# One table for the whole kernel: global queries in batches of four pairs, routed values in pairs of query blocks, gate weights split on the chip

## The chip, the cores and the metric

The kernel runs on one core of one Trainium2 chip. The metric is the time of one execution in device microseconds (us); lower is better. A core has a matrix engine (PE, with PEld for its weight loads), a vector engine (DVE), a scalar engine (ACT), GpSimd (POOL), and DMA queues, of which nearly all are issued from SyncE (SP). Each engine runs its own instructions in the order in which the program lists them, and waits where an input or a buffer is not ready.

## The reference, cut to what matters

Three layers follow each other. First an attention with 512 local and 32 global positions (4 batches, 8 heads of 64): local queries see a band of 32 positions to each side and all global keys, global queries see everything.

```
s_g = scale * np.matmul(q_g, k_all.transpose(0, 1, 3, 2))
out_g = np.matmul(sm(s_g), v_all)
...
a_l = sm(concatenate([s_lg, where(mask, s_ll, -1e9)]))
out_l = np.matmul(a_l, np.concatenate([v_g, v_l], axis=2))
```

Then a routed layer of four causal attention experts (two per token, weighted by a softmax of gate logits), and last a channel mix with a sigmoid gate:

```
scores = where(causal, -1e9, scale * (q @ k.T)); a = softmax(scores)
ye = a @ v @ wo[e]
...
k = np.maximum(xk @ w_k, 0.0)
v = k * k @ w_v
r = 1.0 / (1.0 + np.exp(-(xr @ w_r)))
return (r * v).astype(np.float32)
```

The inputs of `w_k`, `w_v` and `w_r` come as 64-bit floats, and the kernel makes 32-bit ones of them itself.

## The kernel before, in words

Large matrix products are made of three passes in a fast float format (fp32r): each operand is kept as a high part H and a rest L. Small products (scores and values of the attention, values of the experts, transposes) are plain fp32, and each such matmul stands as two records in the trace.

**Attention (tiles S, pn, pT, x).** Sixteen pairs of heads are loaded as `kq` (queries and keys, 688 KB, four buffers) and `vw` (values). `a_qk` makes scores `S` of a half pair in four 64x64 parts of the array, DVE and ACT make the softmax `sm`, POOL scales it to `pn`, PE transposes it (`pT`), and `a_pv` multiplies by the values into `x`. Two pairs make a unit u, two units a batch b. `g_qk(u)` makes the scores `Sga` and `Sgb` of the global queries, four heads side by side in four strips of 32 output partitions; `g_norm` and `g_tp` scale and transpose them into `plg` or `ptlg`. Their product with the values (`xg`) stands inside `a_pv`: every value block that is loaded as weights for `x` serves a 32-column matmul for `xg` too.

**Routed layer (tiles x, pb, pv, C, csm, cT, y, po).** `b_*` project, `c_qk` and `c_norm` make the scaled scores `csm` of one expert pair ep and one block i of 128 queries, `c_tp` transposes them (`cT`) into a buffer `cpt` (two of them), `c_pv` multiplies by the values into `y`, and `e_wo` projects back (`po`). `l_*` do the same for the last 32 positions of all batches.

**Channel mix (tiles m0, m1, k, kk, v, r, rt).** Five tiles of tokens (four of 512, one of 128); per tile 96 matmuls of 512 columns for k, 96 for v and 48 for r. `split_wd` narrows a 64-bit weight chunk with two ACT, one POOL and three DVE instructions, then splits it into H (ACT) and L (POOL). For `w_v` and `w_r` the parts are written to DRAM during the routed layer (`dv..`, `dr..`) and fetched again when their place in SBUF is free (`fetch_wd`).

All calls are first logged; `emit` then issues them by a table of numbers (`ORDER`), and a second table (`SLOTS`) says which buffer each tile takes. So the order on every engine, SP's queue among them, is written out by hand in these tables. The profile has nearly all instructions at the one line of `emit` (L104), so that they are told apart by the names of tiles.

Of the kernel before, what the change touches and what calls it, by code (L numbers as in the profile page):

```python
# [116 lines left out]
def chain_kernel(ctx: ExitStack, tc: tile.TileContext, kq, vw, vgd, wqkv, pack, wo, w_k, w_v, w_r, c_causal, out):  # L117
# [10 lines left out]
    BUFS = {"W0": 1, "W1": 1, "W2": 1, "x": 1, "qk": 3, "kp": 4, "raw": 2, "wy": 2, "wg": 2, "csm0": 4, "csm1": 2,  # L128
            "cpt": 2, "vC": 2, "y": 2, "wo": 2, "pl": 1, "ptl": 1, "rep": 2, "ql": 1}
# [52 lines left out]
    def mm3_rows(ops):  # L182

        for n, (a, x) in enumerate(((1, 3), (1, 4), (2, 3))):
# [8 lines left out]
           for name, k in (("v", 0), ("v", 1), ("r", 0)) for s in "HL"}  # L193
# [22 lines left out]
    def split_wd(name, raw, c, k):  # L216
        lo, hi, hf = raw[:, :, 0], raw[:, :, 1], v32(raw)[:, :, 1]
        y = T("wy", [512], f"wy{name}{c}{k}", U32)
        g = T("wg", [512], f"wg{name}{c}{k}", U32)


# [5 lines left out]
        nc.vector.scalar_tensor_tensor(y, y, 0x7f800000, g, op0=ALU.bitwise_xor, op1=ALU.bitwise_xor)  # L227
        if name == "k":
# [136 lines left out]
    def g_qk(u):  # L365
        sa = ps_s(f"Sga{u}")
        sb_ = ps_s(f"Sgb{u}")
        hs = [(kqs[2 * u + n // 2], slice(64 * (n % 2), 64 * (n % 2) + 64), slice(32 * n, 32 * n + 32)) for n in range(4)]
        for t, rr, oo in hs:
            k = t[rr, KT0:KT0 + 768].rearrange("p (g c) -> p g c", c=96)[:, :, 0:64]  # L370
            nc.tensor.matmul(sa[oo, :], t[rr, QG0:QG0 + SG], k, start=True, stop=True)
        for t, rr, oo in hs:
            nc.tensor.matmul(sb_[oo, 0:SG], t[rr, QG0:QG0 + SG], t[rr, KT0 + 64:KT0 + 96], start=True, stop=True)
        t = pg[u % 2]
        mn = T("mng", [4], f"mng{u}", F32, 2)
        su = T("sug", [1], f"sug{u}", F32, 2)
# [7 lines left out]
    def g_norm(u):
        su = rs.pop(("g", u))
        t = pg[u % 2]
        rc = T("rcg", [1], f"rcg{u}", F32, 2)
# [4 lines left out]
    def g_tp(u):  # L392
        t = pg[u % 2]
        o = ptg[u % 2]
        pT = ps_t(f"pTG{u}")
# [3 lines left out]
        pT2 = ps_t(f"pTh{u}")  # L399
        nc.tensor.transpose(pT2[:, 0:128], t[:, S - 128:S], ident)  # L400
        nc.vector.tensor_copy(o[96:128, NB, :], pT2[96:128, 0:128])

    def a_pv(u):
        b, g = divmod(u, 2)
        pt, pgt, tg = pts.pop(u), ptg[u % 2], tgs.pop(u)
        gp = ps_t(f"xg{u}")
        xs = [ps_x(f"x{u}{pp}") for pp in range(2)]
        for pp in range(2):
            v = vws.pop(2 * u + pp)
            for blk in range(2 * NB):  # L410
                m, c = divmod(blk, 2)
                for h in range(2):
# [16 lines left out]
        nc.vector.tensor_copy(xT[b][:, 2 * g:2 * g + 2, 1:1 + SG], gp[:, 0:64].rearrange("p (a c) -> p a c", a=2))  # L429
# [206 lines left out]
    def l_tp(b):  # L636
# [9 lines left out]
        rr = slice(SG * b, n)  # L646
        nc.vector.tensor_copy(o[rr, NB], pT2[rr, 0:128])
        ptl[b] = o

    yps, yHL = {}, {}  # L650

    def c_pv(b, ep, i):
        if ep == 0 and i == 0:
            yHL[b] = [T("y", [2, S], f"yt{s}{b}", F32R) for s in "HL"]
        if i in (0, NB - 1):
            yps[b, ep] = ps_x(f"y{b}{ep}{i}")
        yp = yps[b, ep]
# [9 lines left out]
        if lastq:  # L667
            for e in range(2):
                hh = 2 * ep + e
                nc.tensor.matmul(yp[64 * e:64 * e + 64, 128:160], v_last[SG * b:SG * b + SG, hh * HD:(hh + 1) * HD],  # L670
                                 ptl[b][SG * b:SG * b + SG, NB, hh * 32:(hh + 1) * 32], start=False, stop=True)
        if i >= NB - 2:
            yH, yL = yHL[b]
            cc, src = (slice(384, S), yp[:, :160]) if lastq else (slice(0, 384), yp[:, :384])
            nc.scalar.copy(yH[:, ep, cc], src)
            nc.vector.tensor_sub(yL[:, ep, cc], src, v32(yH[:, ep, cc]))

    def e_wo(b, c, half):
        yH, yL = yHL[b]
        cc = slice(half * HALF, (half + 1) * HALF)  # L680
        p = ps_t(f"po{b}{c}{half}")
        for ep in range(2):
            mm3(p[:, :HALF], woS[0][:, ep, c * 128:(c + 1) * 128], woS[1][:, ep, c * 128:(c + 1) * 128],
                yH[:, ep, cc], yL[:, ep, cc], ep == 0, ep == 1)
        nc.scalar.copy(xT[b][:, c, 1 + half * HALF:1 + (half + 1) * HALF], p[:, :HALF])
# [194 lines left out]
    jobs += [lambda c=c: load_wd("r", w_r, c, 0, 0) for c in range(NC)]  # L880
    jobs += [lambda c=c: load_wd("k", w_k, c % 4, c // 4, 512 * (c // 4)) for c in range(2 * NC)]
    low = []
    for n in range(NU + 6):
# [27 lines left out]
        if r == 1 and u + 1 < NG:  # L911
# [323 lines left out]
```

## Time and profile before

| | |
|---|---|
| time, median of 3 runs | 516.77 us (515.92 to 517.14) |
| the profiled execution's own time | 515.42 us |
| its span from first to last instruction | 513.6 us |
| mean granted clock of PE | 1.000 |
| PE busy | 499.5 us (97%) |
| PEld, DVE, ACT, POOL busy | 422.1, 312.6, 316.7, 304.8 us |
| DMA | 50.98 MB, HBM read 39.49 MB, written 10.75 MB |

Busy time of PE is the union of matmuls whose ends are modelled and overlap, so a price per matmul is better read from the distance between starts. Idle time of an engine is put down to what ended it.

### The profile page before, as it was taken

To read this page: it belongs to the slowest core of one execution; us is meant where nothing else is said; L and a number is where in the kernel's file an instruction comes from. 1 tells how busy PE (TensorE), PEld (TensorE's weight loads), DVE (VectorE), ACT (ScalarE), POOL (GpSimd) and SP (SyncE) were. 2 spreads that over 40 slices of the span, in tenths; PEclk is the share of its full clock that TensorE was granted. 3 is DMA by queue.
4 is the path that set the end of the run, shared out by engine and by line. 5 is a ranking of instruction groups with operands and counts; after the bars stand their busy time and mean duration, and the time that the engine had idled before them with its cause. 6 is when DMAs were issued, how large, how long until landed. Compare 5 with 4: busy or idle time off the path is not lost.

```text
span 513.6 us, 11622 instructions
## 1 busy us (share of the span) xinstructions
PE 499.5 (97%) x4286; PEld 422.1 (82%) x4286; DVE 312.6 (61%) x1065; ACT 316.7 (62%) x891; POOL 304.8 (59%) x361
## 2 busy tenths in 40 slices
PE   6999999999989999999999999999999999999997
PEld 4777888889969898998888888888888888888885
DVE  5788678768889989999995425303284352301312
ACT  6999787858778797887985556512454264402330
POOL 5978866568759999998896455411484254301321
PEclk9999999999999999999999999999999999999999
DMA  8987452045233543356220020002000110101002
GB/s 341 414 308 271 144 173 75 24 129 202 82 109 139 186 132 99 121 170 241 84 83 1 0 83 1 2 0 83 1 1 0 41 42 0 42 1 42 20 1 82
DMA packets 16024, 50.98 MB, mean 99 GB/s; under 512 B 1760, under 2 KB 2400, under 8 KB 15328
## 3 DMA queue, kind: packets, MB, share of 16 engines
q1 hardware_dynamic: 15680, 49.98, 27.5%
q8 instruction: 34, 0.56, 0.5%
q10 hardware_dynamic: 288, 0.26, 0.1%
q14 instruction: 22, 0.18, 0.1%
HBM read 39.49 MB, written 10.75 MB: 98 GB/s over the span
## 4 chain that ended last, share of the span: by engine, by line
PE 77%; DVE 7%; POOL 6%; ACT 4%; DMA 3%; issue 1%; SPq 0%; POOLq 0%; DVEq 0%; ACTq 0%
PE k L104 18%; PE v L104 18%; PE r L104 9%; PE x L104 5%; PE S L104 3%; PE po L104 3%; PE y L104 3%; PE pv L104 3%; PE pT L104 2%; POOL csm L104 2%; PE cT L104 2%; PE xg L104 2%; PE C L104 2%; PE Sga L104 1%; DVE csm L104 1%
## 5 line engine op out<-in xcount | busy, mean ns | idle before, releaser
L104 POOL TENSOR_TENSOR kk<-k,kk 128x512 fp32r<-128x512 f32 x32 | 43.2, 1357 | 97.2 <-ACT kk L104 94.6
L104 DVE SCALAR_TENSOR_TENSOR mm<-xT,small,mt 128x32 f32<-128x32 f32 (+7 forms) x64 | 48.2, 790 | 46.8 <-POOL m1cpt L104 22.1
L104 DVE TENSOR_TENSOR k<-k 128x512 f32<-128x512 f32 x34 | 27.3, 807 | 74.4 <-ACT k L104 74.1
L104 POOL TENSOR_TENSOR csm<-csm,crc 128x128 f32<-128x128 f32 (+3 forms) x64 | 52.1, 833 | 16.3 <-DVE crc L104 13.8
L104 ACT ACTIVATE sm<-sm,mn 128x160 f32<-128x160 f32 x128 | 53.7, 421 | 10.2 <-DVE mn L104 8.4
L104 POOL TENSOR_TENSOR pn<-sm,rc 128x256 f32<-128x256 f32 x64 | 38.5, 617 | 17.4 <-DVE rc L104 8.6
L104 ACT ACTIVATE k<-k 128x512 f32<-128x512 f32 x34 | 20.1, 597 | 40.7 <-PE k L104 24.0
L104 PE MATMUL v<-wv1H,kk 128*128 128x512 f32 x136 | 44.9, 390 | 0.0
L104 PE MATMUL v<-wv0H,kk 128*128 128x512 f32 x136 | 43.2, 389 | 0.0
L104 ACT ACTIVATE mt<-xT,omu 128x480 f32<-128x480 f32 (+7 forms) x64 | 31.5, 517 | 16.7 <-DVE mm L104 16.6
L104 ACT ACTIVATE csm<-csm,cmn 128x128 f32<-128x128 f32 (+3 forms) x64 | 36.1, 566 | 9.0 <-DVE cmn L104 7.9
L104 DVE CUSTOM_DVE_ANT_0 sm<-S,band 128x160 f32<-128x160 f32 x128 | 35.4, 317 | 9.6 <-PE S L104 7.9
L104 POOL TENSOR_TENSOR m1cpt<-mm,m1vC 128x512 fp32r<-128x512 f32 x16 | 21.4, 1344 | 19.8 <-ACT m1vC L104 18.9
L104 POOL TENSOR_TENSOR m0L<-mm,m0H 128x512 fp32r<-128x512 f32 (+1 forms) x20 | 24.0, 1210 | 14.9 <-ACT m0H L104 12.4
L104 ACT CAST kk<-k 128x512 fp32r<-128x512 f32 x32 | 19.5, 618 | 20.7 <-PE v L104 11.1
L104 DVE CUSTOM_DVE_ANT_0 csm<-C,causal 128x128 f32<-128x128 f32 (+3 forms) x64 | 29.7, 482 | 4.2 <-PE C L104 1.3
L104 PEld LDWEIGHTS v<-wv1H,kk 128*128 128x128 f32 x136 | 25.5, 188 | 5.3
L104 PEld LDWEIGHTS v<-wv0H,kk 128*128 128x128 f32 x136 | 25.5, 188 | 5.3
L104 PEld LDWEIGHTS x<-pt,vw 128*64 128x64 f32 x512 | 24.7, 137 | 5.1 <-issue 1.7
L104 PE MATMUL cT<-ident,csm 128*128 128x128 f32 x160 | 25.3, 280 | 2.9 <-POOL csm L104 2.5
L104 PE MATMUL S<-kq 64*64 64x160 f32 x512 | 23.5, 320 | 4.1 <-DMA kq<-in_kq_dram 4.0
L104 POOL TENSOR_TENSOR x<-xT,x 128x256 fp32r<-128x256 f32 (+1 forms) x32 | 24.3, 780 | 5.1 <-ACT x L104 3.6
(316 smaller groups left out, 1533.7 us busy)
## 6 DMA issues: line engine op xcount, KB each, us to landing
kq<-in_kq_dram SPq DMA_DIRECT2D x15, 688.0 KB, 6.4
vw<-in_vw_dram SPq DMA_DIRECT2D x16, 512.0 KB, 7.3
out_dram<-rt SPq DMA_DIRECT2D x17, 256.0 KB, 2.0
wrawv<-in_moe_w_v_dram SPq DMA_DIRECT2D x8, 512.0 KB, 3.8
wrawk<-in_moe_w_k_dram SPq DMA_DIRECT2D x8, 512.0 KB, 4.3
wrawr<-in_moe_w_r_dram SPq DMA_DIRECT2D x4, 512.0 KB, 3.7
dv0H<-wgv SPq DMA_DIRECT2D x4, 256.0 KB, 3.5
dv0L<-wyv SPq DMA_DIRECT2D x4, 256.0 KB, 2.8
```

The lines of the kernel that those rows point to most:

```text
L104: getattr(getattr(self.nc, engine), name)(*[now(x) for x in args], **{k: now(x) for k, x in kwargs.items()})
```

## The change

Four edits and a new table. `g_qk` takes a whole batch: the two heads of a pair use the two row halves of the array, the four pairs the four strips of output partitions, and there are two score tiles per batch. The product with the values leaves `a_pv` and becomes `g_pv(b)`, with the softmax as weights (32 columns) and the values as the moving side (64 columns); its result has queries on partitions, and one transpose per batch (`pTx`) turns it. `c_tp` and `c_pv` work on two query blocks at a time, 256 or 288 columns. `w_r` is no longer split in the routed layer and sent through DRAM: eight chunks of 256 columns are loaded and split around the first tile of the channel mix, straight into their place. `csm0` has five buffers and `csm1` three; what is set aside of SBUF for software DMA is cut to 1 KB per partition (`dynamic_dma_scratch_size=1024`), which makes room for them.

```
-            "cpt": 2, "vC": 2, "y": 2, "wo": 2, "pl": 1, "ptl": 1, "rep": 2, "ql": 1}
+            "cpt": 2, "vC": 2, "y": 2, "wo": 2, "pl": 1, "ptl": 1, "rep": 2, "ql": 1, "GT": 1}
...
-           for name, k in (("v", 0), ("v", 1), ("r", 0)) for s in "HL"}
+           for name, k in (("v", 0), ("v", 1)) for s in "HL"}
...
+    def load_wr(j):
+        raw = T("csm1", [256, 2], f"wrawr{j}", U32)
+        c, f0 = j // 2, j % 2 * 512
+        nc.sync.dma_start(raw.rearrange("p a b -> p (a b)"), w_r.bitcast(U32)[c * 128:(c + 1) * 128, f0:f0 + 512])
+        return lambda: split_wr(raw, j)
+    def split_wr(raw, j):
+        t = T("wg", [2, 256], f"wyr{j}", U32)
+        y, g = t[:, 0], t[:, 1]
+        narrow(raw, y, g)
+        cc = slice(j % 2 * 256, j % 2 * 256 + 256)
+        H_, L_ = [w[j // 2][:, cc] for w in wd["r", 0]]
+        nc.scalar.copy(H_, v32(y))
+        nc.gpsimd.tensor_sub(L_, v32(y), v32(H_))
...
-        hs = [(kqs[2 * u + n // 2], slice(64 * (n % 2), 64 * (n % 2) + 64), slice(32 * n, 32 * n + 32)) for n in range(4)]
+        hs = [(kqs[NC * b + pp], slice(64 * h, 64 * h + 64), h, slice(32 * pp, 32 * pp + 32)) for pp in range(NC)
+              for h in range(2)]
...
+    def g_pv(b):
+        gp = ps_t(f"xg{b}")
+        v = [vws.pop(NC * b + pp) for pp in range(NC)]
+        for h in range(2):
+            rr = slice(64 * h, 64 * h + 64)
+            for ch in range(NB + 1):
+                blk = 2 * ch if ch < NB else 2 * NB - 1
+                for pp in range(NC):
+                    oo = slice(32 * pp, 32 * pp + 32)
+                    nc.tensor.matmul(gp[oo, rr], ptg[h][:, ch, oo], v[pp][:, blk, rr], start=h == 0 and ch == 0,
+                                     stop=h == 1 and ch == NB, skip_group_check=True)
+        g = T("GT", [128], f"xq{b}")
+        nc.vector.tensor_copy(g, gp[:, 0:128])
+        gT = ps_t(f"pTx{b}")
+        nc.tensor.transpose(gT[:, 0:128], g, ident)
+        nc.vector.tensor_copy(xT[b][:, :, 1:1 + SG], gT[:, 0:128].rearrange("p (a c) -> p a c", a=NC))
...
-                    ch = m if c == 0 else (NB if m == NB - 1 else None)
-                    if ch is not None:
-                        hq = 32 * (2 * pp + h)
-                        nc.tensor.matmul(gp[rr, 32 * pp:32 * pp + 32], w, pgt[:, ch, hq:hq + 32],
-                                         start=pp == 0 and ch == 0, stop=pp == 1 and ch == NB, skip_group_check=True)
...
-        pt = T("cpt", [2, NB, 160], f"cpt{b}{ep}{i}")
+        g, r = divmod(i, 2)
+        if r == 0:
+            cpt[b, ep, g] = T("cpt", [2, NB, 288] if g else [2, 2, 256], f"cpt{b}{ep}{g}")
...
-                nc.tensor.matmul(yp[64 * e:64 * e + 64, o0:o0 + n], vC[b][:, j, hh * HD:(hh + 1) * HD],
-                                 pt[:, e, j, 0:n], start=j == 0, stop=j == i and not lastq)
+                nc.tensor.matmul(yp[64 * e:64 * e + 64, o0:n], vC[b][:, j, hh * HD:(hh + 1) * HD], pt[:, e, j, o0:n],
+                                 start=j == 0, stop=j == i and g == 0, skip_group_check=True)
...
-0 2 14x2 -7 -12 17 -7x2 -15 19 -10 592 -589 -13x2 3x2 10 -19 3 7 -10 152 -152 15 1 171 -177 176 -173x6 92 -93x2 2 -3
+3 6 7x4 -6 -6 584 -593 1x2 -3 2x2 12 2 112 -112 83 -89x2 3x9 3 -4 6x2 -45 11 32x2 -6 5x3 -51 50 -11 -4 13 -14 14 3 -57
```

In all, PE's program has 60 matmuls less: 64 fewer for `y`, and four transposes `pTx` more. The 32 matmuls of `Sga`, the 32 of `Sgb`, the 256 of `x` and the 160 of `xg` keep their number, and so does everything of the channel mix.

What the tables do is seen in the order of instructions. First PE near its start. `Sga0` and `Sgb0` are the global scores of unit 0, `S2`, `S3`, `S4` the local scores of half pairs 2 to 4, `kq0` to `kq3` the loaded pairs. Before:

```order
L104 MATMUL S3_1_191<-kq1_116 64x160
L104 MATMUL Sga0_204<-kq0_84 32x512 x2
L104 MATMUL Sga0_204<-kq1_116 32x512 x2
L104 MATMUL Sgb0_215<-kq0_84 32x32 x2
L104 MATMUL Sgb0_215<-kq1_116 32x32 x2
L104 MATMUL S2_0_223<-kq1_116 64x160
```

and of the change:

```order
L104 MATMUL S4_1_230<-kq2_110 64x160
L104 MATMUL Sga00_245<-kq0_82 32x512
L104 MATMUL Sga01_248<-kq0_82 32x512
L104 MATMUL Sga00_245<-kq1_108 32x512
L104 MATMUL Sga01_248<-kq1_108 32x512
L104 MATMUL Sga00_245<-kq2_110 32x512
L104 MATMUL Sga01_248<-kq2_110 32x512
L104 MATMUL Sga00_245<-kq3_114 32x512
L104 MATMUL Sga01_248<-kq3_114 32x512
L104 MATMUL Sgb00_267<-kq0_82 32x32
L104 MATMUL Sgb01_269<-kq0_82 32x32
L104 MATMUL S6_0_284<-kq3_114 64x160
```

The batch stands behind five half pairs instead of three and needs `kq3`; the buffers of `kq0` to `kq3` are all held until it has run. (Rows of `Sgb` for the other pairs are left out.)

Second PE in the middle of the attention, at the values of batch 1: `x20` is the local result, `xg2` and `xg1` the global one, `plg` the transposed global softmax. Before:

```order
L104 MATMUL x11_778<-tg1_796,vgb_177 128x512
L104 MATMUL x20_858<-pt20_786,vw4_134 64x64
L104 MATMUL xg2_860<-plg_122,vw4_134 64x32
L104 MATMUL x20_858<-pt20_786,vw4_134 64x64 x3
L104 MATMUL xg2_860<-plg_122,vw4_134 64x32
```

and of the change:

```order
L104 MATMUL x20_955<-pt20_857,vw4_639 64x64 x16
L104 MATMUL x21_988<-pt21_922,vw5_629 64x64 x16
L104 MATMUL pT13_1041<-ident_80,pn13_1011 128x128 x4
L104 MATMUL xg1_1051<-vw4_639,plg_87 32x64
L104 MATMUL xg1_1051<-vw5_629,plg_87 32x64
L104 MATMUL xg1_1051<-vw6_649,plg_87 32x64
L104 MATMUL xg1_1051<-vw7_614,plg_87 32x64
L104 MATMUL S18_0_1101<-kq9_735 64x160
```

The matmuls of `x` now follow each other without a break, and the 40 of `xg` stand in one block, in turn over the four strips. (Rows between these are left out; the block's other 36 rows repeat the four.)

Third SP's queue where the routed layer ends: `wrawk` and `wrawr` are 64-bit weights, `dr0H` and `dr0L` the parts of `w_r` in DRAM, `wv..` and `wr..` the fetched parts, `rt03` and `rt00` results of the first tile. Before:

```order
L104 DMA wv0H0_4432<-dv0H_72 128x2048
L104 DMA wv1L0_4605<-dv1L_75 128x2048
L104 DMA wr0H0_4893<-dr0H_76 128x2048
L104 DMA wr0L1_5222<-dr0L_77 128x1024
L104 DMA wr0L0_5229<-dr0L_77 128x1024
L104 DMA out_0_dram<-rt03_5297 128x512
```

and of the change:

```order
L104 DMA wv0H0_4702<-dv0H_72 128x2048
L104 DMA wrawr3_4817<-in_moe2_w_r_dram 128x512
L104 DMA wv1L0_4822<-dv1L_75 128x2048
L104 DMA wrawr4_4927<-in_moe2_w_r_dram 128x512
L104 DMA wrawr2_4951<-in_moe2_w_r_dram 128x512
L104 DMA wrawr5_5123<-in_moe2_w_r_dram 128x512
L104 DMA wrawr7_5130<-in_moe2_w_r_dram 128x512
L104 DMA wrawr6_5163<-in_moe2_w_r_dram 128x512
L104 DMA out_0_dram<-rt00_5410 128x512
```

Three fetches from DRAM have become eight loads of raw weights (two stand further ahead), and four writes each of `dr0H` and `dr0L` in the routed layer are gone.

## Rows read from the trace of the kernel before

**Rows 1.** The page, engines: busy us, share of the span, instructions.

```profile
PE 499.5 (97%) x4286; PEld 422.1 (82%) x4286; DVE 312.6 (61%) x1065; ACT 316.7 (62%) x891; POOL 304.8 (59%) x361
```

**Rows 2.** Waits of PE: engine, tile, releaser; us in total, times, longest.

```profile
PE S L104 <- DMA kq<-in_kq_dram: 4.0, 1, 4.0
PE cT L104 <- POOL csm L104: 2.5, 3, 1.6
PE xg L104 <- ACT ptlg L104: 1.2, 1, 1.2
```

**Rows 3.** Windows: stretch, length, busy of PE, PEld, DVE, ACT, POOL; clock, DMA.

```profile
20.00:100.00 80.00, 79.99 (x1364) 65.36 (x1361) 62.69 (x348) 68.34 (x263) 58.38 (x103) 1.00 0.52 186
160.00:260.00 100.00, 98.47 (x883) 89.38 (x883) 94.17 (x296) 82.58 (x229) 91.49 (x96) 1.00 0.42 143
286.00:326.00 40.00, 40.00 (x196) 33.91 (x195) 14.46 (x21) 24.35 (x49) 19.47 (x14) 1.00 0.08 27
340.00:360.00 20.00, 20.00 (x90) 16.53 (x89) 5.25 (x8) 5.25 (x9) 3.28 (x3) 1.00 0.14 53
```

**Rows 4.** Timeline of PE, 45 to 54 us: start, length, engine, tiles, count of records.

```profile
46.15 1.06 PE L104 MATMUL Sga<-kq 64*32 64x512 f32 x8
47.03 0.24 PE L104 MATMUL Sgb<-kq 64*32 64x32 f32 x8
47.20 0.33 PE L104 MATMUL pTh<-ident,pg 128*128 128x128 f32 x1
47.37 1.04 PE L104 MATMUL pT<-ident,pn 128*128 128x128 f32 x8
...
49.39 0.34 PE L104 MATMUL x<-pt,vw 128*64 128x64 f32 x4
49.56 0.27 PE L104 MATMUL xg<-ptlg,vw 128*64 128x32 f32 x4
49.65 0.48 PE L104 MATMUL x<-pt,vw 128*64 128x64 f32 x8
49.91 0.31 PE L104 MATMUL xg<-ptlg,vw 128*64 128x32 f32 x4
...
50.70 0.36 PE L104 MATMUL x<-pt,vw 128*64 128x64 f32 x4
50.84 0.31 PE L104 MATMUL xg<-ptlg,vw 128*64 128x32 f32 x4
51.08 1.32 PE L104 MATMUL S<-kq 64*64 64x160 f32 x32
52.33 1.06 PE L104 MATMUL Sga<-kq 64*32 64x512 f32 x8
```

**Rows 5.** Timeline of PE in the routed layer, 156 to 160 us.

```profile
156.84 1.31 PE L104 MATMUL y<-cpt,vC 128*64 128x128 f32 x20
158.08 1.48 PE L104 MATMUL C<-qk 64*128 64x512 f32 x12
```

**Rows 6.** The same view, 206 to 212 us.

```profile
208.03 1.31 PE L104 MATMUL y<-cpt,vC 128*64 128x160 f32 x16
209.26 0.30 PE L104 MATMUL y<-ptl,vl 32*64 32x32 f32 x4
```

**Rows 7.** Groups on POOL, shapes apart: count, busy us, mean ns, idle before.

```profile
L104 POOL TENSOR_TENSOR kk<-k,kk 128x512 fp32r<-128x512 f32 x32 | 43.2, 1357 | 97.2 <-ACT kk L104 94.6 <-issue 2.5
...
L104 POOL TENSOR_TENSOR x<-xT,x 128x256 fp32r<-128x256 f32 x16 | 11.4, 730 | 2.1 <-ACT x L104 1.6 <-DVE x L104 0.6
...
L104 POOL TENSOR_SCALAR wyr<-wyr 128x512 f32<-128x512 f32 x4 | 6.4, 1590 | 0.9 <-DVE wgr L104 0.9
L104 POOL TENSOR_TENSOR wyr<-wyr,wgr 128x512 fp32r<-128x512 f32 x4 | 6.1, 1523 | 0.0
```

**Rows 8.** DMA issues: count, KB each, median us from issue to landing.

```profile
kq<-in_kq_dram SPq DMA_DIRECT2D x15, 688.0 KB, 6.4
```

**Rows 9.** Instructions that read `vw`: durations min/median/max ns, first and last start.

```profile
L104 PEld LDWEIGHTS x<-pt,vw x512: 132/138/138, 18.9 to 116.8; 128*64 128x64 f32 x171
```

More of the change, by code (lines that the diff above doesn't have):

```diff
@@ L384, in g_norm, with g_qk @@
[L384 to L387, printed above, removed]
+    def g_qk(b):
+        sa = [ps_s(f"Sga{b}{h}") for h in range(2)]
+        sb_ = [ps_s(f"Sgb{b}{h}") for h in range(2)]
+        hs = [(kqs[NC * b + pp], slice(64 * h, 64 * h + 64), h, slice(32 * pp, 32 * pp + 32)) for pp in range(NC)
+              for h in range(2)]
+        for t, rr, h, oo in hs:
+            k = t[rr, KT0:KT0 + 768].rearrange("p (g c) -> p g c", c=96)[:, :, 0:64]
+            nc.tensor.matmul(sa[h][oo, :], t[rr, QG0:QG0 + SG], k, start=True, stop=True)
+        for t, rr, h, oo in hs:
+            nc.tensor.matmul(sb_[h][oo, 0:SG], t[rr, QG0:QG0 + SG], t[rr, KT0 + 64:KT0 + 96], start=True, stop=True)
+        for h in range(2):
+            t = pg[h]
+            mn = T("mng", [4], f"mng{b}{h}", F32, 2)
+            su = T("sug", [1], f"sug{b}{h}", F32, 2)
+            for c, (o, src) in enumerate(((t[:, 0:SL], sa[h]), (t[:, SL:S], sb_[h][:, 0:SG]))):
+                nc.vector.tensor_tensor_reduce(out=o, in0=src, in1=zcol.to_broadcast([128, o.shape[1]]), op0=ALU.add,
+                                               op1=ALU.min, scale=-SCALE, scalar=BIG, accum_out=mn[:, c:c + 1])
+            nc.vector.tensor_tensor(mn[:, 2:3], mn[:, 0:1], mn[:, 1:2], op=ALU.min)
+            nc.scalar.activation(t, t, AF.Exp, bias=mn[:, 2:3], scale=-1.0, accum_out=su)
+            rs["g", b, h] = su
@@ L668, in c_pv @@
+        if g:
             for e in range(2):
                 hh = 2 * ep + e
[L670 to L676, printed above, removed]
+                nc.tensor.matmul(yp[64 * e:64 * e + 64, 256:288], v_last[:, hh * HD:(hh + 1) * HD],
+                                 ptl[b][:, NB, hh * 32:(hh + 1) * 32], start=False, stop=True,
+                                 skip_group_check=True)
@@ L684, in e_wo @@
                 yH[:, ep, cc], yL[:, ep, cc], ep == 0, ep == 1)
-        nc.scalar.copy(xT[b][:, c, 1 + half * HALF:1 + (half + 1) * HALF], p[:, :HALF])
+        nc.scalar.copy(xT[b][:, c, 1 + t0:1 + t0 + n], p[:, :n])
     def b_groups(b):
@@ L896, in chain_kernel @@
             a_qk(n)
-        if r == 1 and n < NU:
-            g_qk(u)
+        if r == 1 and u % 2 and n < NU:
+            g_qk(u // 2)
         if 0 <= n - 2 < NU:
             a_norm(n - 2)
-        if r == 3 and n < NU:
-            g_norm(u)
+        if r == 3 and u % 2 and n < NU:
+            for h in range(2):
+                g_norm(u // 2, h)
         if 0 <= n - 3 < NU:
             a_tp(n - 3)
-        if r == 0 and 0 < u <= NG:
-            g_tp(u - 1)
+        if r in (0, 1) and u % 2 == 0 and 0 < u <= NG:
+            g_tp(u // 2 - 1, r)
         if r == 2 and 0 < u <= NG:
@@ L910, in chain_kernel @@
             a_pv(u - 1)
-        if r == 1 and u + 1 < NG:
+            if u % 2 == 0:
+                g_pv(u // 2 - 1)
+        if r == (3 if u % 2 == 0 and u > 0 else 1) and u + 1 < NG:
             for P in range(2):
@@ L942, in chain_kernel @@
     for s in "HL":
-        fetch_wd("r", 0, s)
+        place_wd("r", 0, s)
+    parts = [load_wr(0)]
     d_mix(0, 1)
@@ L953, in chain_kernel @@
                     d_k(n, f)
+                if n == 0:
+                    if f + 1 < 2 * NC:
+                        parts.append(load_wr(f + 1))
+                    parts.pop(0)()
                 if f == 2:
@@ new lines @@
+    "wy": "0101010101010101010101011010011011010110011000010111011010",
+    "csm1": "0120121002120121012010210212202112010210121021010100121120201",
+    "cpt": "01010110101010101001011010101010",
+    "wo": "10100101",
+    "wg": "0101010010101011010101010110001001",
+    "qk": "010211102102102",
+    "mn": "01201120012100121022120120121020",
+    "su": "01230312302130212301032310230121",
+    "rc": "01212001210121020212012012012201",
+    "mng": "01010110",
+    "sug": "01011001",
+    "rcg": "01011010",
```

390 lines of the change are left out of this document (185 added, 205 removed).

## Prediction

> **What bounds the kernel now.** I read the engines' busy time first: PE is busy for 97% of the span, the other engines for 59 to 62% [rows 1]. That alone could be an effect of modelled ends, so the waits of PE come next. It waits 4.0 us for its first keys, and the longest waits after that are 2.5 us for `csm`, 1.2 for `ptlg` [rows 2]. The windows say where another engine is close behind: between 20 and 100 us ACT is busy for 68.34 of 80 us, between 160 and 260 us DVE for 94.17 and POOL for 91.49 of 100 [rows 3]. In the channel mix PE issues 90 matmuls of 512 columns in 20 us, 0.222 us each, with the others busy for a quarter or less [rows 3]; none of its matmuls changes. So the time is the length of PE's program plus few waits, and the change is worth what it shortens there, as long as ACT (attention) and DVE and POOL (routed layer) can follow. Prices are distances between starts.
>
> **Global scores.** A batch `Sga` with `Sgb` takes 47.20 - 46.15 = 1.05 us [rows 4], and there are eight: 8.4 us. Now there are four batches of twice as many matmuls. If the eight parts of the array (two row halves, four strips) run side by side, a batch is hardly longer; I add 0.1 us for twice the records, and have 4 x 1.15 = 4.6 us. If only four run at a time, nothing is saved. The nearest row is `S`, on two row halves by two strips: 32 records of 160 columns in 52.33 - 51.08 = 1.25 us, 0.24 ns per record and column, against 0.88 us for 8 x 512 in `Sga`, 0.21 ns [rows 4]. Row halves that share a strip thus do run side by side, four parts at a time. I take the eight: **-3.8 us** (bounds 0 and -4.2).
>
> **Values.** One pair takes 51.08 - 49.39 = 1.69 us [rows 4], and sixteen 27.0 us. In it four records of `xg` cost 0.09 us, the last four 0.24, so a change to another shape costs 0.15; eight records of `x` cost 0.26 and four 0.14, so 0.03 per further record [rows 4]. Alone, the 32 records of `x` cost 0.14 + 28 x 0.03 = 0.98 us, and with a change of shape behind half of them 1.05: 16.8 us. A block of `xg` is 80 records. By the old price per record it costs 80 x 0.0225 = 1.8 us; by columns (an `x` record of 64 columns on two strips 0.0325, on four half of it) 1.3; if no record beats one of `x`, 2.6. I take 1.6, between the two nearest, plus 0.15: 4 x 1.75 = 7.0. The transposes `pTx`: eight `pT` lie 0.96 us apart from the next tile at about 0.13 each [rows 4], with the change of shape 0.2 at most: 0.8. Sum 24.6, **-2.4 us** (bounds: -5.0 with 1.3 and no change of shape behind `x`; +3 with 2.6 and 1.15 for `x`). `pTx` waits for a DVE copy; between `xg` and it stand a half pair of scores or more in PE's order, so I count no wait.
>
> **Values of the experts.** Twenty records of 128 columns take 1.24 us, 62 ns each [rows 5]; sixteen of 160 take 1.23, 77 ns each [rows 6]. The ratio 1.24 is that of the columns, 1.25, so a record is priced by columns, and these stay 1408 per expert pair and head. Merging blocks then saves only ends: 20 stretches of `y` in PE's order become 15, at 0.15 us: **-0.7 us** (bounds 0 and -1). The Trainium skill, TensorEngine Tiling, section Instruction Overhead, says that each matmul carries about 60 cycles of overhead, so that one of a single column takes as long as one of 60. By it as a cost per matmul, 64 fewer with two records each would give 128 x 25 ns = 3.2 us, an estimate from that page; the two rows leave no room for it at 128 columns.
>
> **Gate weights.** In the routed layer the four chunks cost POOL 4 x (1.59 + 1.52) = 12.5 us [rows 7], in the stretch where it is busiest; DVE and ACT are freed of three instructions per chunk as well. PE gains only what it waited for them: up to the 2.5 us of `csm` [rows 2]; I take **-0.5 us**. The eight half chunks come back around the end of the routed layer. The parts L go to the buffers of `wo`, so POOL can't begin before the last `po`. From there to the first `r` it has 14 instructions of 256 columns at 0.73, six `kk` at 1.36 and two mixes of the same width [rows 7]: 10.2 + 8.2 + 2.7 = 21.1 us. PE has 126 matmuls before that `r`, 28.0 us at 0.222. Cover 6.9 us; past it each us of POOL is one of PE. POOL is busy for 19.47 of 40 us there before [rows 3], so it fits. SP has eight loads for three fetches and no write to wait for.
>
> **Buffers and table.** One buffer more for each of `csm0` and `csm1` lets scores run further ahead, at no work. A new order can remove PE's waits or make others; of the 1.2 us for `ptlg` [rows 2], I count half, since `xg` now comes after other work: **-0.6 us** (bounds: all 3.7 us of these two waits gone, or as much new).
>
> **Sum.** 3.8 + 2.4 + 0.7 + 0.5 + 0.6 = 8.0 us. The profiled execution's 515.42 (513.6 of span, 1.8 around it) becomes 507.4; the median of the runs shown is 1.35 above that execution, so the forecast is 516.77 - 8.0 = **508.8 us**.
>
> **Rivals.**
> - *Strips less parallel* (faster, by less). No more than four parts of the array at a time, or `xg` at 2.6 us a block. For it: no row has eight parts. Against it: `S`, above. Time 516.77 - 4.2 = 512.6, or with both about 514.
> - *ACT paces the attention* (about no change). Between 20 and 100 us it is busy for 68.34 of 80 [rows 3]. Shortened by the five sixths of 6.2 us that fall there, that is 68.34 of 74.8, 91%. Against it: 9% are left, and PE had none of its own. If none of the 6.2 us is realised: 515.0; with a little of the rest lost too, the same as before.
> - *The key buffers* (slower). Four buffers of `kq` are held until the batch has run, then the next pairs load, 6.4 us to landing [rows 8], where before two came free at a time. After batch 0 the order has three half pairs of `S` at 0.62 us, four groups of transposes at 0.48 and one `x` of 0.98 before `S9` needs `kq4` [rows 4]: 4.8 us, so up to 1.6 us of wait; after batch 1 about 8 us, none. If the loads came late by the whole 6.4 us three times, 19 us would be lost: 516.77 - 8.0 + 19 = 528. It decides from 2.7 us per batch. Against it: ACT is still busy with the scores of earlier half pairs then.
> - *Weight loads in series* (slower). A weight load lasts 138 ns [rows 9]. If those of `xg`, whose four strips use all 128 rows, had to wait for the array, a block would cost 80 x 0.138 = 11 us, and the time would be 516.77 - 8.0 + 4 x 9.4 = 546. The Trainium skill, TensorE: Matmul & The Clock Gate, section What overlaps and what doesn't, has loads overlap running matmuls only where row groups differ. By that rule `x` would take 512 x 0.138 = 71 us; it takes 16 x 1.09 = 17 us [rows 4, 9], so the trace does not agree.
> - *The waits go too* (faster, by more). With POOL and DVE relieved and more buffers, the 3.7 us of `csm` and `ptlg` and a block of `xg` at 1.3: 503 to 505.
>
> **How the numbers follow.** What a measurement of this kernel can tell from no change is about 0.2%, 1.0 us. Forecast (505.5 to 512) 0.62; strips 0.12; waits gone 0.09; ACT 0.07 (about half of it within 0.2%); key buffers 0.08 (0.06 slower, 0.02 the same); weight loads 0.02. Faster 0.86, same 0.06, slower 0.08. The range 503.5 to 514.0 takes in the strips and most of the last rival, and leaves out ACT, the slow ones and the lower end.
>
> **What would show it.** In the profile after: `Sga` with `Sgb` at 1.1 to 1.2 us per batch, not 2.1; a block of 80 records of `xg` at 1.3 to 1.9 us; 32 records of `x` in 1.0; `y` at 0.48 ns per column and record; no wait of PE for `kq` after the first over 2 us; none of `r` for POOL; ACT at about 90% between 20 and 95 us. The prediction is wrong if PE's list of waits grows by several us, with `kq`, ACT or POOL as releaser, or if blocks on four strips run no faster than on two.

## The result: 504.97 us, 2.3% faster

| | before | after |
|---|---|---|
| median, us | 516.95 (515.92 to 517.35, 4 runs) | 504.97 (504.69 to 505.24, 4 runs) |
| profiled execution: own time, span | 515.42, 513.6 | 505.11, 503.3 |
| PE: busy, records | 499.5 of 513.6, 4286 | 490.8 of 503.3, 4162 |

The ratio of the runs is 0.9771, with an interval of 0.9754 to 0.9788; the medians are 12.0 us apart. The forecast was 508.8, the range 503.5 to 514.0; the likeliest case's own range (505.5 to 512) is missed by half a microsecond. The two profiled executions are 10.3 us apart, since that of before lay 1.5 us under its median; what follows accounts for those 10.3.

The line of the engines' busy time answers to [rows 1]:

```profile
PE 490.8 (98%) x4162; PEld 410.4 (82%) x4162; DVE 299.3 (59%) x1077; ACT 314.6 (62%) x903; POOL 300.0 (60%) x373
```

PE's list of waits (total, times, longest) begins so and answers to [rows 2]:

```profile
PE S L104 <- DMA kq<-in_kq_dram: 5.3, 2, 4.0
PE xg L104 <- DVE ptlg L104: 0.7, 2, 0.5
PE pTG L104 <- DVE mn L104: 0.6, 1, 0.6
```

The wait for `csm` is gone, that for `ptlg` is smaller, and there is a second one for keys (1.3 us), which the profile of before does not have. The windows answer to [rows 3]; the stretch from 5 to 50 us is added, and is told below:

```profile
20.00:100.00 80.00, 77.90 (x1429) 62.60 (x1424) 61.92 (x350) 70.00 (x274) 59.37 (x103) 1.00 0.56 201
160.00:260.00 100.00, 99.58 (x825) 87.58 (x825) 83.84 (x291) 81.43 (x230) 81.34 (x95) 1.00 0.26 91
...
5.00:50.00 45.00, 42.30 (x821) 30.76 (x813) 36.61 (x232) 42.58 (x172) 34.39 (x60) 1.00 0.88 327
```

In the routed layer PE is now busy for 99.58 of 100 us (98.47 before), and DVE and POOL have come down by 10 us each. In the attention it has gone the other way: 77.90 of 80 us instead of 79.99.

PE's timeline, the second batch and the block of `xg` ahead of it, answers to [rows 4]:

```profile
25.18 0.77 PE L104 MATMUL xg<-vw,plg 128*32 128x64 f32 x40 [0.50 <-DVE ptlg L104]
25.76 0.74 PE L104 MATMUL xg<-vw,ptlg 128*32 128x64 f32 x40
26.43 1.32 PE L104 MATMUL S<-kq 64*64 64x160 f32 x32
27.68 1.15 PE L104 MATMUL x<-pt,vw 128*64 128x64 f32 x32
28.76 0.33 PE L104 MATMUL pTx<-ident,xq 128*128 128x128 f32 x1
28.93 0.60 PE L104 MATMUL pT<-ident,pn 128*128 128x128 f32 x4
29.46 1.09 PE L104 MATMUL Sga<-kq 64*32 64x512 f32 x16
30.34 0.27 PE L104 MATMUL Sgb<-kq 64*32 64x32 f32 x16
30.54 0.75 PE L104 MATMUL S<-kq 64*64 64x160 f32 x13
```

By distances between starts, a batch of eight tiles takes 30.54 - 29.46 = 1.08 us (forecast 1.15; four tiles took 1.05), a block of 80 records of `xg` 1.25 (1.75), 32 records of `x` 1.08 (1.05), `pTx` 0.17 (0.2). The third batch did not run through:

```profile
49.08 1.77 PE L104 MATMUL Sga<-kq 64*32 64x512 f32 x12
50.24 0.26 PE L104 MATMUL Sgb<-kq 64*32 64x32 f32 x6
50.67 0.61 PE L104 MATMUL Sga<-kq 64*32 64x512 f32 x4
51.57 0.28 PE L104 MATMUL Sgb<-kq 64*32 64x32 f32 x10 [0.29 <-issue]
51.77 1.15 PE L104 MATMUL x<-pt,vw 128*64 128x64 f32 x32
```

It takes 51.77 - 49.08 = 2.69 us. Its last two loads of keys were asked for at 41.44 us only: SP had stood since 32 us at the load of `rawwv`, whose buffer came free at 41.06, and those two stood behind it.

Summed over all records of a tile, from the start of each to the start of PE's next record, the 10.3 us are: scores `Sga`, `Sgb` 8.9 to 5.9 (-2.9), `x` by `vw`, `xg` and `pTx` 28.6 to 23.4 (-5.1), `y` 27.0 to 21.9 (-5.2), `cT` 21.0 to 18.4 (-2.6), `pT` and `pTg` -1.4; and against that `S` 22.5 to 25.6 (+3.0), `pTh` 1.2 to 2.6 (+1.4), `x` by `tg` +0.9, the 512-column matmuls of the mix 232.1 to 233.5 (+1.4). So 17 us went, in matmuls and in waits, and nearly 7 came back, most of it before 113 us.

Part of what came back is not the change's. The kernel before has been profiled once more, without `w_r` (below); its attention is the same program, and there it has the second wait for keys too:

```profile
8.12 1.34 PE L106 MATMUL S<-kq 64*64 64x160 f32 x16 [1.66 <-DMA kq<-in_kq_dram]
```

In that profile `S` takes 24.4 us and the attention ends 2.6 us later than in the one of before that is compared here. Like with like, both with this wait, `S` is 1.2 us longer by the change, and the last `x` by `tg` starts 7.1 us earlier (120.3 to 113.2), not 4.5.

### The profile page after: what moved, and what is told of

Its sections match the earlier page's. It is cut to its first block, busy times and chain, and to the rows that moved or that the text cites. A ratio compares the mean times of both kernels' runs of the same rounds, so it can differ in the third digit from the quotient of the medians.

```text
span 503.3 us, 11352 instructions
## 1 busy us (share of the span) xinstructions
PE 490.8 (98%) x4162; PEld 410.4 (82%) x4162; DVE 299.3 (59%) x1077; ACT 314.6 (62%) x903; POOL 300.0 (60%) x373
## 3 DMA queue, kind: packets, MB, share of 16 engines
q1 hardware_dynamic: 14672, 45.78, 25.6%
## 4 chain that ended last, share of the span: by engine, by line
PE 77%; DVE 8%; ACT 6%; DMA 4%; issue 2%; POOL 1%; SPq 0%; POOLq 0%; ACTq 0%
PE k L104 18%; PE v L104 16%; PE r L104 8%; PE pv L104 4%; PE po L104 4%; PE x L104 3%; PE S L104 3%; PE y L104 3%; PE cT L104 3%; DMA kq<-in_kq_dram 3%; PE C L104 2%; ACT sm L104 2%; PE pT L104 2%; DVE csm L104 1%; DMA rawwo<-in_moe_wo_dram 1%
## 5 line engine op out<-in xcount | busy, mean ns | idle before, releaser
L104 POOL TENSOR_TENSOR kk<-k,kk 128x512 fp32r<-128x512 f32 x32 | 41.2, 1296 | 60.5 <-ACT kk L104 58.6
L104 DVE SCALAR_TENSOR_TENSOR mm<-xT,small,mt 128x96 f32<-128x96 f32 (+7 forms) x64 | 40.1, 646 | 49.6 <-POOL m0L L104 18.9
L104 POOL TENSOR_TENSOR csm<-csm,crc 128x128 f32<-128x128 f32 (+3 forms) x64 | 50.3, 800 | 20.2 <-DVE crc L104 14.7
L104 DVE TENSOR_TENSOR k<-k 128x512 f32<-128x512 f32 x34 | 26.1, 779 | 51.3 <-ACT k L104 51.3
L104 POOL TENSOR_TENSOR pn<-sm,rc 128x256 f32<-128x256 f32 x64 | 38.3, 614 | 20.3 <-DVE rc L104 10.8
L104 POOL TENSOR_TENSOR m0L<-mm,m0H 128x512 fp32r<-128x512 f32 (+1 forms) x20 | 22.5, 1128 | 33.7 <-ACT m0H L104 33.7
L104 DVE CUSTOM_DVE_ANT_0 sm<-S,band 128x160 f32<-128x160 f32 x128 | 35.6, 316 | 10.3 <-PE S L104 6.9
L104 ACT ACTIVATE mt<-xT,omu 128x448 f32<-128x448 f32 (+7 forms) x64 | 32.1, 518 | 12.2 <-DVE mm L104 12.2
L104 DVE TENSOR_TENSOR rt<-v,rt 128x512 f32<-128x512 f32 x17 | 11.5, 688 | 34.5 <-ACT rt L104 19.4
L104 DVE CUSTOM_DVE_ANT_0 csm<-C,causal 128x384 f32<-128x384 f32 (+3 forms) x64 | 30.2, 487 | 2.2 <-POOL csm L104 1.3
L104 PE MATMUL S<-kq 64*64 64x160 f32 x512 | 25.2, 326 | 5.4 <-DMA kq<-in_kq_dram 5.3
L104 PEld LDWEIGHTS v<-wv0H,kk 128*128 128x128 f32 x136 | 25.6, 188 | 5.5
L104 POOL TENSOR_TENSOR x<-xT,x 128x256 fp32r<-128x256 f32 (+1 forms) x32 | 24.4, 775 | 4.4 <-ACT x L104 2.6
L104 PE MATMUL pv<-wv,x 128*128 128x260 f32 x192 | 26.6, 288 | 0.0
```

What stands on the lines that cost most here:

```text
L104: getattr(getattr(self.nc, engine), name)(*[now(x) for x in args], **{k: now(x) for k, x in kwargs.items()})
```

## The experiments

My theory after the comparison: eight tiles do run side by side; half of what the attention earned in the two profiles went into waits, made by SP's order or by ACT; and the routed layer gained less from columns than from relief of POOL, DVE and ACT and from fewer changes of a tile's shape. The kernel before ran beside every group of runs, at medians of 516.7 to 517.4 us with single runs from 514 to 520.6, so an interval is some 1.5 us to either side; below that the rows decide.

**Eight tiles or four.** The batch's code, in the changed kernel:

```diff
+        for part in (hs[:NC], hs[NC:]):
-        for t, rr, h, oo in hs:
+            for t, rr, h, oo in part:
...
-            nc.tensor.matmul(sa[h][oo, :], t[rr, QG0:QG0 + SG], k, start=True, stop=True)
+                nc.tensor.matmul(sa[h][oo, :], t[rr, QG0:QG0 + SG], k, start=True, stop=True)
```

> The changed kernel, with each batch of global scores issued as two groups of four tiles, every group's Sgb ahead of the next group's Sga; so no more than four tiles have work at a time, and nothing else differs. Theory (eight tiles run side by side, and this is where 3 us of PE's program went): a batch takes about 2.1 us from the start of its Sga to the next tile instead of 1.08, 4 us more in all, and the time is about 508.5 to 509, unless the third batch hides some of it in its wait for keys (then 508). Rival (the gain came from fewer changes between tiles and from the order, not from eight tiles at once): a batch stays at 1.1 to 1.4 us, time 505 to 506.

Measured: 505.96 us, ratio 0.978 (0.9744 to 0.9816), as the changed kernel. The forecast of 508.5 fell, but not for the reason that the rival gives. PE's timeline of this run, the first batch and the third:

```profile
12.36 1.12 PE L104 MATMUL Sga<-kq 64*32 64x512 f32 x16
13.25 0.29 PE L104 MATMUL Sgb<-kq 64*32 64x32 f32 x16
...
50.12 1.06 PE L104 MATMUL Sga<-kq 64*32 64x512 f32 x8
51.01 0.24 PE L104 MATMUL Sgb<-kq 64*32 64x32 f32 x8
52.85 1.06 PE L104 MATMUL Sga<-kq 64*32 64x512 f32 x8 [1.60 <-DMA kq<-in_kq_dram]
```

In the first batch all sixteen records of `Sga` start ahead of any `Sgb`, though the program has four matmuls of `Sga`, four of `Sgb`, four and four: the division did not take place, and it did not in the second and fourth either. In the third, the keys held the second group back, and so this one batch is the test: four tiles take 51.01 - 50.12 = 0.89 us for `Sga`, eight in the first batch 13.25 - 12.36 = 0.89 too. Eight tiles cost what four cost.

**Where `y` got cheaper.** Two edits of the changed kernel, one each:

```diff
-    nc.tensor.matmul(..., v_last[:, hh * HD:(hh + 1) * HD], ptl[b][:, NB, hh * 32:(hh + 1) * 32], ...)
+    nc.tensor.matmul(..., v_last[SG * b:SG * b + SG, ...], ptl[b][SG * b:SG * b + SG, NB, ...], ...)
```
```diff
-    nc.tensor.matmul(yp[64 * e:64 * e + 64, o0:n], vC[b][...], pt[:, e, j, o0:n], ...)
+    cuts = [(o0, 128), (128, n)] if o0 == 0 else [(128, n)]      # one matmul per cut and head
```

> The changed kernel, with the last matmul of each head of y (ptl by v_last) again on 32 rows of the array instead of 128, as in the kernel before. Columns and records are the same. Theory (y became 2.5 us cheaper beyond its lost waits because a change of the tile's shape costs PE about 0.1 to 0.15 us, and the kernel before had eight to sixteen more of them): 1.2 to 1.6 us more, 506.2 to 506.6. Rival (y is priced by columns alone and the rest was hidden waits): no more than 0.2 us, 504.8 to 505.2.

> The changed kernel, with every wide matmul of y (256 or 288 columns) issued as one of 128 and one of the rest, inside the same stretch; 64 matmuls more, the columns the same. Theory (priced by columns): 0 to 0.4 us more, 505.0 to 505.4. Rival (about 60 cycles, 25 ns, of overhead for each record, the rule of the Trainium skill, TensorEngine Tiling, section Instruction Overhead): 128 records more, 3.2 us more, about 508.2.

Measured: 506.58 us (0.9798, 0.9767 to 0.983) and 505.46 (0.9777, 0.9742 to 0.9812). In the second, the sums of `y` are not the reference's, since each piece sets its own start; the work is the same. PE's timeline of the changed kernel, and under it of the run with 32 rows, at the same place:

```profile
141.73 1.95 PE L104 MATMUL y<-cpt,vC 128*64 128x288 f32 x16
143.51 0.26 PE L104 MATMUL y<-ptl,vl 128*64 128x32 f32 x4
143.69 0.97 PE L104 MATMUL cT<-ident,csm 128*128 128x128 f32 x5
```
```profile
142.56 1.95 PE L104 MATMUL y<-cpt,vC 128*64 128x288 f32 x16
144.43 0.30 PE L104 MATMUL y<-ptl,vl 32*64 32x32 f32 x4
144.67 0.82 PE L104 MATMUL cT<-ident,csm 128*128 128x128 f32 x5
```

The change of rows costs 0.09 us ahead of the four records (1.87 instead of 1.78) and 0.06 behind; over all `y` the sum is 23.0 us instead of 21.9. That supports the theory at its lower end; the time alone doesn't tell it from nothing. For the records cut in two, the same place in the changed kernel and in the run:

```profile
218.53 0.87 PE L104 MATMUL y<-cpt,vC 128*64 128x256 f32 x8
219.33 0.96 PE L104 MATMUL C<-qk 64*128 64x512 f32 x6
```
```profile
217.63 0.88 PE L106 MATMUL y<-cpt,vC 128*64 128x128 f32 x12
218.44 0.97 PE L108 MATMUL C<-qk 64*128 64x512 f32 x6
```

Eight records take 0.80 us, the twelve that replace them 0.81, and the sum over all `y` is 22.0 us beside 21.9. 128 records more cost 0.1 us. The rule of the Trainium skill (TensorEngine Tiling, Instruction Overhead), taken as a cost per matmul, would by estimate have made them 3.2 us and the ratio 0.983; the trace does not agree with it at 128 columns. At these widths `y` is priced by columns and by changes of shape.

**SP's order.** The loads of buffers ten and eleven ahead of `rawwv`; in the second run also, at the start, the third key buffer's behind `small`:

```diff
+        load = [n for n in order if self.ops[n][:2] == ("sync", "dma_start")]
+        for first, then in [(24, 23), (25, 23)]:      # second run: also (3, 5)
+            order.remove(load[first])
+            order.insert(order.index(load[then]), load[first])
```

> The changed kernel, with the loads of the key buffers ten and eleven issued by SP ahead of rawwv, which waits for its buffer until 41 us and holds them back. Theory (the wait of 1 us inside the third batch and the wait for ACT-fed work around it come from SP's order, not from a lack of buffers): the two loads are issued several us earlier, PE's wait for kq in Sga is gone, and 0.5 to 1.5 us of the time: 503.5 to 504.5. Rival 1 (the buffers come free no earlier): same as the changed kernel, 505.0. Rival 2 (ACT is the pacer in this stretch, and waits only move): PE's wait for kq goes, others grow, 504.7 to 505.2.

> The changed kernel, with two edits of SP's order: the loads of key buffers ten and eleven ahead of rawwv, and at the start the load of the third key buffer behind small, as in the kernel before. Theory (both waits come from SP's order): PE's second wait for kq of 1.3 us at 6.4 us shrinks to 0.3 or less, the third batch of global scores runs through in 1.1 to 1.5 us instead of 2.7, no other wait takes it up; 1 to 2 us less than the changed kernel, 503 to 504. Rival 1 (ACT or DVE follow so closely that waits only move): the two waits go, others between 10 and 100 us grow by as much, 504.5 to 505.2. Rival 2 (the keys land late because four loads and the values share the DMA engines, not because of their order): the wait at 6.4 us stays at 1 us or more.

> The changed kernel itself, once more, on the chip of the three runs beside it. 504.5 to 505.5 us; ratio to the kernel before 0.976 to 0.978. Its spread is what the others are read against.

Measured: 505.11 us (0.9774, 0.9742 to 0.9807) with the first edit; with both 505.0 (0.9787, 0.9759 to 0.9815), beside 506.39 (0.9802, 0.9774 to 0.983) for the changed kernel on the same chip. In the first run the third batch takes 1.54 us instead of 2.69, so the wait for its keys did come from SP's order. But that order does not always cost it. In the second profile of the changed kernel the same two loads, asked for at 42.0 and 42.5 us, had landed by 48.7, and the batch took 2.16 us all the same:

```profile
49.05 1.09 PE L104 MATMUL Sga<-kq 64*32 64x512 f32 x16
49.93 0.23 PE L104 MATMUL Sgb<-kq 64*32 64x32 f32 x6
51.00 0.28 PE L104 MATMUL Sgb<-kq 64*32 64x32 f32 x10 [0.84 <-issue]
51.21 1.15 PE L104 MATMUL x<-pt,vw 128*64 128x64 f32 x32
```

PE stands ahead of the last ten records of `Sgb` there, and the profile does not show what for. And in the first run another wait for keys, of 1.42 us, stands at 20.3 us, ahead of the place that the edit moves; the run with the batch divided has one of 1.24 us there. The second wait for keys, at 6.4 us, is not settled by it: with the order unchanged it is 1.30 and 1.49 us in the two profiles of the changed kernel, 1.66 in the first run here, and absent in those with `y` in pieces and with more work in the routed layer. With both edits the third batch takes 1.55 us, and PE's waits begin so:

```profile
PE S L109 <- DMA kq<-in_kq_dram: 4.5, 2, 4.2
PE pT L109 <- POOL pn L109: 2.0, 3, 1.5
```

The keys are there, and PE waits 1.5 us for the first weights `pn` instead. Rival 1 fits: the waits move. The spans are 502.6 and 502.7 us beside 503.3 and 503.4, so the two edits may give up to 0.8 us; the times can't tell. The forecasts of a gain (503.5 to 504.5, 503 to 504) were missed.

**Who paces the start.** ACT without its sums:

```diff
-    nc.scalar.activation(ts[:, h, i], ts[:, h, i], AF.Exp, bias=mn[:, c:c + 1], scale=-1.0, accum_out=su[:, c:c + 1])
+    nc.scalar.activation(ts[:, h, i], ts[:, h, i], AF.Exp, bias=su[:, c:c + 1], scale=-1.0)   # su: the minima
```

> The changed kernel, without the sums of the local softmax: ACT's exponentials accumulate nothing, and the minima are taken in the sums' place; so the weights are not those of the reference. ACT is freed of its reads of the accumulators in the attention, some 20 us of its busy time before 110 us. Theory (attention now waits for buffers, keys and the order, 3 to 4 us, with ACT never the one that comes last): PE's waits in the attention change by less than 1 us, 504 to 505.5. Rival (ACT, busy for 70 of 80 us, paces the attention, and this ate half of what PE's shorter program earned there): PE's waits before 110 us shrink by 2 us or more, 501 to 503.

Measured: 502.91 us (0.9747, 0.9716 to 0.9778), span 500.9, on the chip on which the changed kernel took 506.39 and 503.4. The window from 5 to 50 us of this run:

```profile
5.00:50.00 45.00, 42.78 (x877) 31.65 (x869) 37.47 (x242) 39.11 (x111) 36.57 (x63) 1.00 0.89 347
```

In the changed kernel ACT is busy there for 42.58 of 45 us, 95%, and from 6 to 20 us for 13.70 of 14. With a third fewer instructions on ACT, PE gets on: the third batch starts at 46.46 us instead of 49.08. Not all of these 2.6 us are ACT's, since the second wait for keys is absent here. It is absent too in four other runs with the same attention. In three of them (`y` in pieces; POOL or DVE loaded, below) the third batch starts at 48.35, 47.86 and 47.81 us, so that ACT's part is 1.4 to 1.9; at the last `x` by `tg` it is 1.1 to 1.9 (110.3 us against 111.4 to 112.2). The fourth, with all three engines loaded, starts the batch at 49.56: its matmuls are slow for longer at the start (16 records of `S` from 10.59 us on take 1.35 us, in the changed kernel 0.77 from 11.03 on). So the rival holds by half: ACT paces the first 50 us, and behind them nothing more is gained.

**Relief of the routed layer, from before.** The kernel before, with `w_r`'s loads (four in this kernel, not eight), arithmetic and writes not issued:

```diff
+        nc.skip = name == "r"            # around the load, the arithmetic and the writes
...
-                    nc.sync.dma_start(v32(t), wdr[name, k, s][:, c:c + m])
+                    nc.sync.dma_start(v32(t), wdr["v" if name == "r" else name, k, s][:, c:c + m])
```

> The kernel before, without the gate weights' split: their eight loads, their arithmetic on ACT, DVE and POOL and their writes to DRAM are left out, and the channel mix fetches parts of w_v in their place, so the mix computes with wrong gate weights; PE's program and every fetch stay. Theory (about half of what the routed layer gained, 7.5 us before its last po, came from relieving POOL, DVE and ACT of the four chunks): PE's waits for csm and in front of cT and y shrink, 2 to 4 us less than before, 513 to 515, and its last po comes 2 to 4 us earlier than 298.8. Rival 1 (the prediction's term): 0.5 us, 516.2 to 516.6. Rival 2 (the order of before, made with that work in it, has no place for the gain): nothing, 516.7.

Measured: 515.46 us, ratio 0.9952 (0.9928 to 0.9977): 2.5 us less by the ratio, 1.2 to 3.7, and 1.5 by the medians (516.97 beside it). The rows of `x` and `po` (first and last start) of before, and under them of this run, bound the routed layer:

```profile
L104 PE MATMUL x<-tg,vgb x32: 589/641/694, 22.5 to 117.7; 64*128 64x512 f32 x32
...
L104 PE MATMUL po<-ytH,woL x64: 282/288/296, 160.2 to 298.8; 128*128 128x272 f32 x64
```
```profile
L106 PE MATMUL x<-tg,vgb x32: 588/642/694, 25.0 to 120.3; 64*128 64x512 f32 x32
...
L106 PE MATMUL po<-ytH,woL x64: 282/288/295, 162.0 to 298.8; 128*128 128x272 f32 x64
```

From the last `x` to the last `po` it is 181.1 us before and 178.5 here, 2.6 less, with PE's program untouched: the theory. Its other sign, a last `po` 2 to 4 us earlier, did not come, and the span is 513.7 us: the attention of this profile was 2.6 us longer, by the second wait for keys and what followed it. Such a delay gives the other engines time, too; how much of the 2.6 us comes of that, the rows can't tell. The times, of 12 runs beside 29, bear out 1.2 us or more. In the list of waits `cT` for `csm` goes from 2.5 us to 1.6 only. The run takes work off three engines and the DMA queues at once and does not divide them.

**The same in reverse, in the changed kernel.** Steps of the split of `w_v` repeated: POOL's twice, DVE's three times, or both with ACT's three times.

```diff
         nc.gpsimd.tensor_scalar(v32(y), v32(y), TINY, None, op0=ALU.max)
+        if more:
+            nc.again(2)                  # the step above is emitted twice
```

> The changed kernel, with single steps of the split of w_v repeated to no effect in the routed layer: about 12 us more on POOL, 11 on DVE and 11 on ACT, about what the change took from POOL there, and more than it took from DVE and ACT. Theory (lost waits in the routed layer, 2.5 us in cT and csm and 2.5 in y, came from relieving POOL and DVE of the gate weights): PE's waits come back, 2.5 to 5 us more, 507.5 to 510. Rival (they came from one more buffer for each of csm0 and csm1 and from the new order): less than 1 us more, 505 to 506.

> The changed kernel, with POOL's step of the split of w_v done twice in the routed layer, eight times 1.6 us, about 12 us more, near to what the change took from POOL there; DVE and ACT as they are. With all three engines loaded it lost 21 us. Theory (POOL is the engine on whose slack the routed layer depends): 5 us or more lost, 510 or more. Rival (the loss came from DVE, or from the three in a chain, ACT to POOL to DVE): less than 2 us, 505 to 507.

> The changed kernel, with DVE's last step of the split of w_v done three times in the routed layer, about 11 to 25 us more on DVE by the 0.7 to 1.7 us that such a step of 512 columns takes; POOL and ACT as they are. Theory (DVE, at 84 of 100 us the busiest engine beside PE in the routed layer, has the least slack): most of the 21 us of the run that loaded all three, 515 or more. Rival (POOL was it): less than 4 us lost, 505 to 509.

Measured: 526.74 us (1.0201, 1.0171 to 1.0231) for all, 20 us over the changed kernel on the same chip, where the forecast was 2.5 to 5; 515.62 (0.9961, 0.9935 to 0.9986) for POOL, 515.48 (0.9969, 0.9944 to 0.9993) for DVE, by the ratios each 8 to 10 us over the changed kernel. Both forecasts for single engines came true in number (510 or more, 515 or more), and so neither engine is the one that the routed layer depends on: neither has room for this work. The first place shows how 3 us become 4. POOL's timeline of the changed kernel and of the run with POOL loaded:

```profile
117.56 3.13 POOL L104 TENSOR_SCALAR wyv<-wyv 128x512 f32<-128x512 f32 x2 [0.22 <-ACT wyv L104]
```
```profile
117.17 6.28 POOL L108 TENSOR_SCALAR wyv<-wyv 128x512 f32<-128x512 f32 x4 [0.21 <-ACT wyv L108]
```

Then a wait of DVE in that run, PE's timeline, and windows with the granted clock behind the busy times:

```profile
DVE wyv L108 <- POOL wyv L108: 3.1, 2, 1.8
```
```profile
122.81 1.61 PE L108 MATMUL pv<-wv,x 128*128 128x260 f32 x12
127.16 2.90 PE L108 MATMUL pb11q<-x,wq 128*128 128x256 f32 x12 [2.74 <-DVE qk L108]
129.86 0.63 PE L108 MATMUL cT<-ident,csm 128*128 128x128 f32 x2
```
```profile
124.00:128.00 4.00, 1.26 (x8) 1.05 (x7) 3.97 (x13) 2.27 (x6) 2.77 (x4) 0.90 0.62 197
127.20:130.60 3.40, 3.40 (x16) 3.07 (x18) 1.80 (x7) 1.59 (x5) 1.57 (x2) 0.50 0.51 181
```

POOL is 3.1 us longer, DVE (which waits for it in its own order) comes late with `qk`, PE waits 2.7 us, and behind that wait the granted clock is 0.50 from 127.2 to 130.6 us, the lower of its levels of 1.2 and 2.4 GHz: `pb11q`'s twelve records take 2.70 us from start to start, where the same shape takes 1.42 elsewhere (`pb11k`, 117.10 to 118.52 us of this run). This wait is thus paid for twice. With DVE loaded the granted clock is 0.50 from 150.8 to 157.6 us, around and behind a wait of 1.82 us. The kernel before does not pay so for its longest wait for `csm`, 1.64 us at 152.8 us: the granted clock is 1.00 from 150 to 156 us. So of the 8 to 10 us of a single engine up to 1.7 (POOL) and 3.4 (DVE), half of the stretch at 0.50, are the clock's.

## Why the prediction was right, by its steps

The direction, the bound (PE's program plus few waits) and the range held. The sum was 8.0 us against 10.3 in the profiles and 12.0 in the medians, and that it came so near is luck in part: the first term was too high, the next three were too low, the last has no settled sign, and the profile of before had no second wait for keys.

- *Global scores, -3.8.* The mechanism is shown: 1.08 us per batch, four tiles and eight alike. Three batches follow it; the third lost 1.6 us, to keys that came late by SP's order and to a wait ahead of `Sgb`. Measured -2.9.
- *Values, -2.4.* Right in kind; the term was mis-sized, by `xg`: 1.25 us per block is the price by columns (1.3), the lower bound, not the middle. By the prediction's own base of 27.0 us, 16 x 1.08 + 4 x 1.25 + 4 x 0.17 = 23.0: -4.0; over all records -5.1.
- *Values of the experts, -0.7.* The price by columns is shown, and the overhead per matmul excluded at these widths, by the run with 64 matmuls more. But the term left out that the last matmul of each head now has 128 rows like its neighbours: 1.1 us by the run with 32. `y` lost 5.2 us. Of these, six stretches of `y` fewer in PE's order (20 to 14), and so six ends, are 1.2, a wait of 0.7 for `csm` behind `y` is gone, and in the run without `w_r` `y` takes 0.9 less than before, so relief may give that much. Some 1.3 stay open.
- *Gate weights, -0.5.* The step that was furthest off in kind: it let PE gain only what stood in the list of waits under `csm`, 2.5 us, and took a fifth of it. The relief was worth 2.5 us in the kernel before (1.2 to 3.7), with only 0.9 of it in that row, and 12 us put back on POOL cost 8 to 10. The cover at the mix was right: no wait of `r` for POOL.
- *Buffers and table, -0.6.* Mis-sized, and in the two profiles of the other sign: the waits for `csm` went, but `S` (+3.0) and `pTh` (+1.4) took 4.4 us before 113 us. Of these, 1.8 go with the second wait for keys, which comes and goes in both kernels (`S` 22.5 and 24.4 us in the two profiles of before). ACT costs 1.1 to 1.9, and SP's order at most 1.1, at the third batch. The undoing of the two added buffers was not tried, since the new order keeps more of them in use at once than the old count holds; what they are worth stays open.
- *The rivals.* The time is that of *the waits go too* (503 to 505), half by its mechanism: `csm`'s waits gone, `xg` at 1.25. *ACT paces the attention* is true of the first 50 us and costs 1.1 to 1.9 us there; the window that I read, from 20 to 100 us, hid it at 85%. *Key buffers*: in the profile of the result the wait came at the third batch, by SP's order. Where the rival had it, behind the first batch, it came in two other profiles: 1.42 and 1.24 us, with 6.8 and 6.6 us from issue to landing of those keys (4.9 in the result's). *Strips less parallel* and *weight loads in series* are excluded by the rows of `Sga` and `xg`. The first of these was also added up wrongly: with both of its conditions the terms leave 8.0 - 3.8 - 4.0 = 0.2 us, so 516.6 us and not about 514.

## What to carry to other kernels

Read the waits of the engine that bounds, but don't price relief of its suppliers by one row of that list alone: here work taken off them gave 1.2 to 3.7 us where the row shrank by 0.9, and 12 us of work put on POOL, busy for 81% of the stretch, cost 8 to 10, with the order on each engine fixed. Look for the pacer in windows short enough. In the kernel before, ACT is busy for 85% of the 80 us that the prediction read, and for 92% (41.48 of 45 us) of these:

```profile
5.00:50.00 45.00, 43.52 (x777) 31.95 (x769) 36.98 (x217) 41.48 (x164) 33.86 (x58) 1.00 0.92 354
```

When several tiles need several loads at once, go through the DMA queue's order for one load that waits for its buffer ahead of theirs. And before a new wait is put down to a change, see whether another profile of the kernel before has it too.

## What was not expected of the hardware

That each engine runs its instructions in the order of the program, as was said at the start, is not so for PE: its records do not always start in program order when they go to different parts of the array. In the divided batch sixteen records of `Sga` start within 0.53 us ahead of the first `Sgb`, though eight `Sgb` records stood between them, and in the third batch of the changed kernel six of `Sgb` start (50.24 us) ahead of the last four of `Sga` (50.67). As far as these rows go, a matmul that stands for a busy part does not hold back one for a free part; no run here was made to test that alone. A change of 32 to 128 rows and back costs 0.15 us in the rows of `y`, though no wait shows it.
